# 32-step triangular inverses from two 16-step blocks in one lane, joined by small TensorE products

## The chip, the cores and the metric

The kernel runs on one core of a Trainium2 chip. The metric is the device time of one execution in microseconds (us), the median of several runs. Engines are named as in the profile: PE (TensorE matmul), PEld (its weight load), DVE (VectorE), ACT (ScalarE), POOL (GpSimd), SP (SyncE, which issues the DMAs).

## The reference, cut to what matters

```python
# 32 (batch, head) pairs, 768 steps, state 40 x 40, float32
for t in range(S):
    y[:, :, t] = einsum('bhd,bhde->bhe', r_t, state)
    Sa = einsum('bhde,bhe->bhd', state, a_t)
    state = state * w_t[:, :, None, :] - einsum('bhd,bhe->bhde', Sa, b_t) + einsum('bhd,bhe->bhde', v_t, k_t)
x = y as (3072 tokens, 320)
h = x @ w_in                                  # 320 -> 1024
solu = h * softmax(h)
x = layer_norm(solu) * g_ln @ w_out           # 1024 -> 320
h = x @ w2_in                                 # 320 -> 2048
out = (max(h, 0) + alpha * min(h, 0)) @ w2_out
```

The recurrence is computed in chunks of 32 steps. Within a chunk the update by `a` and `b` couples the steps, which makes a strictly lower triangular 32 x 32 matrix L for each chunk and head, and the kernel needs -(I + L)^-T of it. This inverse is what the change rewrites.

## The kernel before, in words

**Two phases.** `phase1` runs over 24 chunks of 32 steps (a slot each, `slot(g)`), two chunks to a window of 64 steps, and puts the first pair of products (the layers "h", "ptr", "po", "ptx") of earlier tokens between the chunks' own products. A second phase does the second pair of products (L1016 to L1039) and isn't touched.

**One slot.** In PE's order: `px` (L429), `pu` (L442, `stage_u`), `pf` (L465, `stage_uf`), `pst` (L477), `pg` (L520), `pss` (L497 or L500), `py` (L540), and between them the pieces of a queue of layer products: h (L575), ptr (L614), po (L628 to L630), ptx (L642). Each slot also prepares later windows: scans of the decays on DVE (L273 to L286, L277), scaled operands (L303 on DVE or POOL), XS (L312 on POOL), transposes pt (L401), and `gen1` (L326), which makes the matrices that become XS (L336) and L (L339, an ACT copy out of PSUM). For the first slots it decodes weight words: DVE L656 to L662, ACT L658 and L659, POOL L665, then an ACT cast L692.

**The inverse.** Four consecutive chunks (g//4 is the same) make 128 units of 32 x 32, (head, chunk) pairs, a unit to a lane. `inverse(W)` (L343 to L393) makes their inverses: a DVE transpose (L366) puts each unit into one partition, 31 rank-1 steps follow (L354 a multiplication into `tmp`, L358 an addition; L383 for the smallest ones), and a second transpose (L387) puts the result back into LMN, from where `pu` and `pf` read it as weights. W=0 is made ahead of slot 0, there with the rows from 10 on done by POOL (L354 and L358 on POOL). W+1 is made in the slots with g%4 = 2 and 3 (`inv_tasks`, first 18 pieces and the rest) and read from the next slot on. So there are six inverses: one ahead of slot 0, and one in each of the slot pairs 2/3, 6/7, 10/11, 14/15 and 18/19.

**What sets the order.** PE's order is that of the code. `pace` follows how many columns the array has lately worked on, by the code's own estimates, and where the count falls under a floor (`LEVELS`) takes a piece from the queue of layer products (`pop`); with an empty queue it takes a product of zeros: "busy" (L211, 128x512) in slots 0 to 3, "zero" (L182) later. `keep(24)` in slot 0 puts 24 "busy" products ahead of `pu`; the first waits for a memset of `busy` (L945), which is tied behind step KSTEP = 20 of the first inverse. The order of DVE, ACT, POOL and SP is set by the framework's scheduler, which weighs when operands are due; each engine then runs its list in order.

Of the kernel before, what the change touches and what calls it, by code (L numbers as in the profile page):

```python
# [21 lines left out]
KEEP0, KEEP1, KSTEP, KEND = 36, 24, 20, 4  # L22
# [10 lines left out]
PR, SM, TM = (10, 32), 2, 121  # L33
# [6 lines left out]
NI = 18  # L40
# [8 lines left out]
def tile_kernel(ctx: ExitStack, tc: tile.TileContext, w_fm, a0_fm, a_fm, kb_fm, r_fm, v_fm, v_tm,  # L49
                w1_in, w1_out, g_ln, w2_in, w2_out, alpha, ident_d, mask_d, r, k, v, w, a, b, w1_nat, out,  # L50
# [138 lines left out]
    def pace(dt, n):  # L189
        """follows dt us in which the array counts n columns: keeps those of the last SPAN us above the floor"""  # L190
        note(dt, n)
        floor, extra = LEVELS[min(st["slot"] // 4, 1) if st["slot"] != 4 else 2] if st["slot"] < NG - 4 else LEVELS[3]
# [4 lines left out]

    def idle(dt):
        """dt us in which the next products wait for other engines"""
        while dt > 0.1 and more():  # L200
            dt -= pop()
        note(max(dt, 0.0), 0)
# [39 lines left out]
    def check(w, pe):  # L242
        """counts what is out of range"""
# [70 lines left out]
    def gen1(g, half):  # L314
# [16 lines left out]
        c4, lraw = g % 4, st["lraw"]  # L331
# [11 lines left out]
    def inverse(W):  # L343
        M, NT = LMN[2 * W % 3], LMN[(2 * W + 1) % 3]

        P = PR[W > 0]

        def rank1(eng, tmp, s, rows):
            nt = 31 - s
            l = NT[:, s + 1:32, s]  # L350
            tv = tmp[:, 0:sum(b - a for a, b in rows) * nt].rearrange("p (i t) -> p i t", t=nt)
            for a, b in rows:
                sh = [128, b - a, nt]
                eng.tensor_tensor(out=tv[:, a - rows[0][0]:b - rows[0][0]], in0=M[:, a:b, s:s + 1].to_broadcast(sh),  # L354
                                  in1=l.unsqueeze(1).to_broadcast(sh), op=ALU.mult)
            for a, b in rows:
                o = M[:, a:b, s + 1:32]
                r = eng.tensor_tensor(out=o, in0=o, in1=tv[:, a - rows[0][0]:b - rows[0][0]], op=ALU.add)  # L358
            return r

        def pool_rows():
            for s in range(P, 31):
                rank1(nc.gpsimd, b1.tile([128, TM], F32, name="tmp2", tag="Yt"), s, [(P, s + 1)])

        def start():
            nc.vector.transpose(out=NT, in_=st["lraw", W].rearrange("p l t -> p t l"))  # L366
            if W:
                unit(M, nc.gpsimd)
            pool_rows()

        def step(s):
            n, nt = min(s + 1, P), 31 - s
            m = n // 2
            if n <= SM:
                ops = [(M[:, i, s + 1:32], NT[:, s + 1:32, s], M[:, i, s:s + 1]) for i in range(n)]
            elif nt <= SM:
                ops = [(M[:, 0:n, s + 1 + i], M[:, 0:n, s], NT[:, s + 1 + i, s:s + 1]) for i in range(nt)]
            else:
                st["step"] = rank1(nc.vector, b1.tile([128, 256], F32, name="tmp"), s,
                                   [(0, m), (m, n)] if W == 0 else [(0, n)])  # L380
                return
# [67 lines left out]
    def blank(p):  # L449
        """zeros in the rows between those of the two heads"""  # L450
# [201 lines left out]
    def decode(raw, e, m, o, scales=()):  # L652
        """scales: of column ranges, a factor for each row"""
# [14 lines left out]
    def words(src, scales=()):  # L668
        """words of 256 columns a row, or of 512 while the layers' tiles are free, decoded"""
# [126 lines left out]
    def inv_tasks(g):  # L796
# [26 lines left out]
    def tail_tasks(g):  # L823
        """of the tokens after the last chunk: transposes in, first products, second ones, transposes out"""
# [19 lines left out]
    def slot(g):  # L844
# [72 lines left out]
    def phase1():  # L917
# [8 lines left out]
        nc.sync.dma_start(out=mask, in_=mask_d)  # L926
        nc.sync.dma_start(out=ident, in_=ident_d)
# [13 lines left out]
        for i, (_, f) in enumerate(inverse(0)):  # L941
# [40 lines left out]
    def phase2(p2):  # L982
# [12 lines left out]
        def parts(f):  # L995
            """of the weights of 128 hidden units: the three row tiles in, and the rows out"""
# [52 lines left out]
        def limits():  # L1049
            """whether a decay is out of range"""  # L1050
# [202 lines left out]
    with ExitStack() as ms:  # L1253
# [99 lines left out]
```

## Time and profile before

| what | us |
|---|---|
| median of 3 runs (lowest to highest) | 1180.27 (1178.73 to 1182.65) |
| span of the profiled execution, first to last instruction | 1174.9 |
| PE busy in the span | 994.3 (85%) |
| DVE busy | 794.3 (68%) |
| ACT busy | 516.9 (44%) |
| POOL busy | 503.1 (43%) |
| mean granted TensorE clock | 0.896 |

The profile is of one execution, for which it gives the span from the first to the last instruction; the median of the runs is 5.4 us above it. In the rows, a timeline line is start, duration, engine, line, operation, what it writes and reads, count and, in brackets, how long the engine had been idle and which instruction ended that. A matmul of fp32 operands has two records, so 32 products of `pu` stand as x64. [...]

### The profile page before, as it was taken

How to read it: one execution, taken by the hardware profiler on the slowest of the kernel's cores; microseconds unless marked ns; L12 is line 12 of the kernel's file. 1: busy time of each engine (PE TensorE's matmuls, PEld its weight loads, DVE VectorE, ACT ScalarE, POOL GpSimd, SP SyncE). 2: the span in 40 equal slices, each digit the busy share in tenths (PEclk: the TensorE clock that was granted, in tenths of full speed). 3: DMA queues.
4: the chain of work that ended last, by engine and by line, in shares of the span. 5: the costliest groups of instructions: out<-in, count | busy, mean ns of one | idle time of the engine just before them, and what ended most of it. 6: DMA issues, size and time to landing. Idle time of an engine off the chain costs nothing.

```text
span 1174.9 us, 37092 instructions
## 1 busy us (share of the span) xinstructions
PE 994.3 (85%) x15913; PEld 802.3 (68%) x15934; DVE 794.3 (68%) x1610; ACT 516.9 (44%) x1198; POOL 503.1 (43%) x546
## 2 busy tenths in 40 slices
PE   6275686588878978797779878999999999999997
PEld 3233454467666767676667666788888888888886
DVE  8899689978988798879878966556333333333332
ACT  3324454476547663666465647655212121212121
POOL 6848565444434433443444326245233333333332
PEclk8676877789888987888889889999999999999999
DMA  5513344434333433343334333445202020201000
GB/s 167 140 43 94 82 145 123 105 108 126 86 93 107 125 78 93 107 125 78 96 89 119 106 90 94 119 144 169 55 1 73 1 73 1 72 1 48 1 23 15
DMA packets 105423, 100.24 MB, mean 85 GB/s; under 512 B 38244, under 2 KB 84644, under 8 KB 105252
## 3 DMA queue, kind: packets, MB, share of 16 engines
q1 hardware_dynamic: 105252, 97.80, 30.1%
q8 instruction: 127, 2.08, 0.8%
q14 instruction: 44, 0.36, 0.1%
HBM read 72.34 MB, written 25.43 MB: 83 GB/s over the span
## 4 chain that ended last, share of the span: by engine, by line
PE 44%; DVE 32%; ACT 6%; issue 6%; POOL 5%; DMA 5%; SPq 0%; POOLq 0%; DVEq 0%; ACTq 0%
PE ph L1016 13%; PE acc L1037 5%; DVE tmp L354 5%; PE acc L1039 5%; PE acc L1038 5%; DVE LMN L358 4%; PE h L575 4%; DMA kbf<-in_kb_fm_dram 3%; DVE VUS L482 2%; DVE KBS L508 2%; PE ph L1019 2%; DVE XS L336 2%; DVE H L277 2%; DVE P L582 1%; PE pf L465 1%
## 5 line engine op out<-in xcount | busy, mean ns | idle before, releaser
L1026 POOL TENSOR_TENSOR gll<-gt,gh 128x512 fp32r<-128x512 f32 (+1 forms) x112 | 127.1, 1153 | 239.0 <-ACT gh L1025 219.8
L595 DVE TENSOR_SCALAR gt<-ph,al 128x512 f32<-128x512 f32 (+1 forms) x112 | 71.1, 670 | 219.5 <-PE ph L1019 218.0
L1025 ACT CAST gh<-gt 128x512 fp32r<-128x512 f32 (+1 forms) x112 | 61.1, 560 | 268.9 <-DVE gt L596 268.6
L575 PE MATMUL h<-w1h,xt 128*128 128x512 f32 x240 | 104.4, 483 | 16.3 <-ACT h L584 16.3
L312 POOL TENSOR_TENSOR XS<-XS,H 40x512 f32<-40x512 f32 (+1 forms) x48 | 64.9, 1356 | 89.6 <-DVE H L277 53.7
L354 DVE TENSOR_TENSOR tmp<-LMN,LMN 128x87 f32<-128x87 f32 (+25 forms) x189 | 93.5, 506 | 3.4
L1037 PE MATMUL acc<-w2h,gh 128*128 128x320 f32 x288 | 94.0, 326 | 0.0
L1039 PE MATMUL acc<-w2h,gll 128*128 128x320 f32 x288 | 89.1, 309 | 0.3 <-POOL gll L1026 0.3
L1038 PE MATMUL acc<-w2l,gh 128*128 128x320 f32 x288 | 88.9, 309 | 0.0
L211 PE MATMUL busy<-busy 128*128 128x512 bf16 x200 | 61.8, 463 | 28.1 <-DVE tmp L354 22.9
L528 POOL TENSOR_TENSOR YS<-YS,mask 64x512 f32<-64x512 f32 x48 | 64.3, 1339 | 47.6 <-ACT YS L527 42.9
L358 DVE TENSOR_TENSOR LMN<-LMN,tmp 128x87 f32<-128x87 f32 (+25 forms) x189 | 77.1, 419 | 2.7
L575 PEld LDWEIGHTS h<-w1h,xt 128*128 128x128 f32 x240 | 50.0, 219 | 25.8 <-ACT h L584 18.5
L575 PE MATMUL h<-w1l,xt 128*128 128x512 f32 x144 | 67.5, 469 | 0.0
L628 PE MATMUL po<-wo1h,lnh 128*128 128x320 f32 x192 | 66.7, 348 | 0.5 <-DVE lnl L620 0.5
L596 DVE SCALAR_TENSOR_TENSOR gt<-ph,gt 128x512 f32<-128x512 f32 (+1 forms) x112 | 63.9, 606 | 0.5
L630 PE MATMUL po<-wo1h,lnl 128*128 128x320 f32 x192 | 61.5, 320 | 0.2 <-DVE lnl L620 0.2
L629 PE MATMUL po<-wo1l,lnh 128*128 128x320 f32 x192 | 61.5, 320 | 0.0
L211 PEld LDWEIGHTS <-busy 128*128 128x128 bf16 x221 | 23.2, 114 | 55.0 <-DVE busy L945 22.6
L1037 PEld LDWEIGHTS acc<-w2h,gh 128*128 128x128 f32 x288 | 54.1, 188 | 9.6 <-issue 7.4
L581 ACT ACTIVATE P<-h,sm 128x1024 f32<-128x1024 f32 x24 | 26.7, 1114 | 69.0 <-DVE sm L580 65.8
L1016 PE MATMUL ph<-w1h,w2h 128*128 128x512 f32 x180 | 56.6, 396 | 0.0
(214 smaller groups left out, 2718.9 us busy)
## 6 DMA issues: line engine op xcount, KB each, us to landing
kbf<-in_kb_fm_dram SPq DMA_DIRECT2D x24, 416.0 KB
x2d<-x SPq DMA_DIRECT2D x24, 320.0 KB
xd<-Y SPq DMA_DIRECT2D x24, 256.0 KB
xt<-xd SPq DMA_DIRECT2D x12, 512.0 KB
raw<-in_w_in_dram SPq DMA_DIRECT2D x20, 256.0 KB
wt<-in_w_fm_dram SPq DMA_DIRECT2D x24, 211.7 KB
raw<-in_w_in_dram SPq DMA_DIRECT2D x8, 512.0 KB
raw<-in_w_out_dram SPq DMA_DIRECT2D x16, 256.0 KB
```

What stands on the lines that cost most here:

```text
L211: nc.tensor.matmul(st["busy"], lhsT=busy[:, 0:128], rhs=busy, start=True, stop=True)
L312: (nc.vector if w < 2 and e in DA else nc.gpsimd).tensor_tensor(out=o, in0=o, in1=h, op=ALU.mult)
L354: eng.tensor_tensor(out=tv[:, a - rows[0][0]:b - rows[0][0]], in0=M[:, a:b, s:s + 1].to_broadcast(sh), in1=l.unsqueeze(1).to_broadcast(sh) ...
L358: r = eng.tensor_tensor(out=o, in0=o, in1=tv[:, a - rows[0][0]:b - rows[0][0]], op=ALU.add)
L575: nc.tensor.matmul(st["h"][:, ns], lhsT=l, rhs=r, start=j == 0, stop=j == len(ops) - 1)
L595: nc.vector.tensor_scalar(out=tmp, in0=h, scalar1=0.0, scalar2=al, op0=ALU.min, op1=ALU.mult)
L628: nc.tensor.matmul(po, lhsT=lh[:, k], rhs=wo1h[:, k], start=k == 0, stop=False)
L1016: nc.tensor.matmul(p, lhsT=l, rhs=r, start=j == 0, stop=False)
L1026: nc.gpsimd.tensor_tensor(out=gll, in0=t, in1=f32(gh), op=ALU.subtract)
L1037: nc.tensor.matmul(acc, lhsT=gh[:, cs], rhs=oh, start=f == 0, stop=False)
L1038: nc.tensor.matmul(acc, lhsT=gh[:, cs], rhs=ol, start=False, stop=False)
L1039: nc.tensor.matmul(acc, lhsT=gll[:, cs], rhs=oh, start=False, stop=f == K2 - 1)
```

## The change

The 32 x 32 triangle is cut into two diagonal blocks of 16 and the block between them. ACT writes L into a new tile GR (L339). Two half-size DVE transposes (L352, L353) bring both diagonal blocks of a unit into one lane of LMN. There, 14 steps work on both blocks at once, in place (L360 a multiplication, L363 an addition; 28 to 112 elements a lane). A masked copy (L368), a memset (L369) and a transpose (L370) make VT, and an ACT instruction (L371) VR from it. Then PE forms, per unit, `pv` (L376, 32x16 results, 128 of them), which ACT copies to A (LMN[2], L386), and `pn` (L376 too, 32x32 results, 128 of them), which ACT copies in two halves to LMN (L392), where `pu` reads the inverse. The first 16 pieces of `inverse` (all DVE work) go into the slot with g%4 = 2, the four PE pieces (left, left, join, join) into the slot with g%4 = 3; in slot 0 they stand between `keep(24)` and `stage_u`. POOL no longer takes rows of the first inverse. The memset that releases `keep(24)` is tied to step 2 instead of 20. A DMA of a constant `tri` (164 KB) and three POOL copies of it in `init` are new, and the memsets of LMN are gone.

```diff
-KEEP0, KEEP1, KSTEP, KEND = 36, 24, 20, 4
+KEEP0, KEEP1, KSTEP, KEND = 36, 24, 2, 4
...
     def init():
-        unit(LMN[0], nc.gpsimd)
+        for t, c, k in ((GR, 0, 0), (VR, 0, 1), (LMN[2], 16, 2)):
+            i = tri[:, 256 + 16 * k:272 + 16 * k].unsqueeze(1).to_broadcast([128, 32, 16])
+            nc.gpsimd.tensor_copy(out=t[:, :, c:c + 16], in_=i)
...
-                nc.scalar.activation(out=lraw[r:r + 32, c4 * 8:c4 * 8 + 8, :], in_=pg[o + 32:o + 64, :, e],
+                nc.scalar.activation(out=GR[r:r + 32, c4 * 8:c4 * 8 + 8, 47:15:-1], in_=pg[o + 32:o + 64, :, e],
                                      func=AF.Copy, scale=-1.0)
...
     def inverse(W):
+        X = LMN[W % 2]
+        L = X[:, 0:16, :].rearrange("p t (b a) -> p b t a", b=2)
+        A = LMN[2]
+        box = {}
 
         def start():
-            nc.vector.transpose(out=NT, in_=st["lraw", W].rearrange("p l t -> p t l"))
-            if W:
-                unit(M, nc.gpsimd)
-            pool_rows()
+            nc.vector.transpose(out=X[:, 15::-1, :], in_=GR[:, :, 32:48].rearrange("p l c -> p c l"))
+            nc.vector.transpose(out=X[:, ::-1, 16:32].rearrange("p s c -> p c s"),
+                                in_=GR[:, :, 16:32].rearrange("p l c -> p c l"))
 
         def step(s):
+            sh = [128, 2, 15 - s, s]
+            tmp = b1.tile([128, 128], F32, name="tmp")[:, 0:2 * s * (15 - s)]
+            tmp = tmp.rearrange("p (b t a) -> p b t a", b=2, a=s)
+            nc.vector.tensor_tensor(out=tmp, in0=L[:, :, s + 1:16, s:s + 1].to_broadcast(sh),
+                                    in1=L[:, :, s:s + 1, 0:s].to_broadcast(sh), op=ALU.mult)
+            o = L[:, :, s + 1:16, 0:s]
+            st["step"] = nc.vector.tensor_tensor(out=o, in0=o, in1=tmp, op=ALU.add)
 
         def fin():
-            st["fence"] = nc.vector.transpose(out=NT.rearrange("p l t -> p t l"), in_=M.rearrange("p i t -> p t i"))
-            st["NT", W] = NT
...
+            nc.vector.tensor_tensor(out=V.rearrange("p (b t) a -> p b t a", b=2), in0=L, in1=low, op=ALU.mult)
+            nc.vector.memset(V.rearrange("p (b t) a -> p b (t a)", b=2)[:, :, ::17], 1.0)
+            st["fence"] = nc.vector.transpose(out=VT.rearrange("p l a -> p a l"), in_=V.rearrange("p x a -> p a x"))
+            nc.scalar.activation(out=VR[:, :, 31:15:-1], in_=VT, func=AF.Identity, scale=tri[:, 320:321])
+
+        def units(p, lhsT, rhs, rows, ls):
+            for l in ls:
+                for q in range(0, 128, 32):
+                    nc.tensor.matmul(p[q:q + 32, l - ls[0], :], lhsT=lhsT[q:q + rows, l, 0:32], rhs=rhs[q:q + rows, l, :],
+                                     start=True, stop=True)
+                pace(0.11, 16)
+
+        def left(h):
...
+            units(p[:, 16 * h:16 * h + 16], GR, VT, 16, range(16 * h, 16 * h + 16))
+            if h:
+                nc.scalar.copy(out=A[:, :, 0:16], in_=p)
+
+        def join(h):
...
+            units(p, A, VR, 32, ls)
+            nc.scalar.copy(out=X[:, 16 * h:16 * h + 16, :], in_=p)
...
-        inv = [f for _, f in inverse(W + 1)]
-        return inv[:NI] if c4 == 2 else inv[NI:]
+        inv = list(inverse(W + 1))
+        return inv[:16] if c4 == 2 else inv[16:]
...
             keep(KEEP1)
+            for f in st["joins"]:
+                f()
         stage_u(g)
```

PE's program grows from 10256 to 12136 instructions: 768 `pv` and 768 `pn`, "zero" from 15 to 115 and "busy" from 221 to 293 (34 more in slot 0, 38 more in slot 3), their weight loads among them. Each of the slots 7, 11, 15 and 19 has 25 "zero" products where it had none.

**Place 1: PE in slot 0**, from `px` to `pf` (XP is the copy of `px`, LMN_161 and LMN_160 the tiles of the inverse). Before:

```order
L429 MATMUL px<-VUS_163,XS_150 32x40 x32
L211 MATMUL busy<-busy 128x512
...
L442 MATMUL pu<-XP,LMN_161 32x40 x4
...
L442 MATMUL pu<-XP,LMN_161 32x40 x28
L451 MATMUL pf<-D_148 32x256
```

Now:

```order
L376 MATMUL pv<-VT,GR 32x16 x4
...
L376 MATMUL pv<-VT,GR 32x16 x68
...
L376 MATMUL pv<-VT,GR 32x16 x56
L376 MATMUL pn<-VR,LMN_162 32x32 x12
...
L376 MATMUL pn<-VR,LMN_162 32x32 x68
...
L376 MATMUL pn<-VR,LMN_162 32x32 x48
L450 MATMUL pu<-XP,LMN_160 32x40 x16
```

Between the `keep(24)` and `pu` now stand the 128 `pv` and 128 `pn`, and where "..." stands among them 8 or 9 "busy" products of `pace`, 35 in all.

**Place 2: ACT in slot 0**, behind the copy of `px` (L666, L667 and L700 are the decode lines L658, L659 and L692 of before). Now:

```order
L440 COPY XP<-px 128x320
L371 ACTIVATE VR<-VT,tri 128x32x16
L251 ACTIVATE H,flags<-wt,lims 104x8x64 x2
L386 COPY LMN_162<-pv 128x32x16
L666 ACTIVATE wem<-wem,ebias 128x512
L667 ACTIVATE wem<-wem 128x512
L251 ACTIVATE H,flags<-wt,lims 104x8x64 x2
L700 CAST w1h<-wem 128x512
...
L392 COPY LMN_160<-pn 128x512
...
L392 COPY LMN_160<-pn 128x512
L454 COPY VUS_167<-pu 32x320
```

Before, the copy of `px` was followed by two decode instructions (L658, L659) and the copies of `pu`; now the three copies of the inverse stand among range checks (L251), decode instructions and casts.

**Place 3: DVE in slots 6 to 8**, the end of an inverse and the next window's scans (Yt is the result of a slot, XS the next operand). Before, ahead of slot 8's `pu`:

```order
L383 SCALAR_TENSOR_TENSOR LMN_161<-LMN_161,LMN_162 128x31
L387 STREAM_TRANSPOSE LMN_162<-LMN_161 128x32x32
L273 TENSOR_SCALAR wc<-wt 104x8x64
L274 MEMSET wc 104x9
L281 SCALAR_TENSOR_TENSOR F<-wc,D_148 104x520
```

Now, the end of the inverse is ahead of slot 6's Yt, and the scans ahead of slot 7's:

```order
L363 TENSOR_TENSOR LMN_160<-LMN_160,tmp 128x2x14
L368 TENSOR_TENSOR V<-LMN_160,tri 128x512
L369 MEMSET V 128x2x16
L370 STREAM_TRANSPOSE VT<-V 128x16x32
...
L552 TENSOR_TENSOR Yt<-py,H 104x512
...
L490 TENSOR_TENSOR VUS_167<-pst,VUS_168 40x320 x4
L273 TENSOR_SCALAR wc<-wt 104x8x64
...
L277 SCALAR_TENSOR_TENSOR H<-wc,Dx 104x520
...
L552 TENSOR_TENSOR Yt<-py,H 104x512
```

DVE's part of the inverse has moved from two slots into the first of them, and the scans from the beginning of slot 8 into slot 7.

## Rows read from the trace of the kernel before

**Rows 1.** The page: the chain that ended last, by engine and by line

```profile
PE 44%; DVE 32%; ACT 6%; issue 6%; POOL 5%; DMA 5%; SPq 0%; POOLq 0%; DVEq 0%; ACTq 0%
PE ph L1016 13%; PE acc L1037 5%; DVE tmp L354 5%; PE acc L1039 5%; PE acc L1038 5%; DVE LMN L358 4%; PE h L575 4%; DMA kbf<-in_kb_fm_dram 3%; DVE VUS L482 2%; DVE KBS L508 2%; PE ph L1019 2%; DVE XS L336 2%; DVE H L277 2%; DVE P L582 1%; PE pf L465 1%
```

**Rows 2.** Instructions by line, DVE: count, busy us, mean ns, idle before

```profile
L354 DVE TENSOR_TENSOR tmp<-LMN,LMN 128x87 f32<-128x87 f32 (+25 forms) x189 | 93.5, 506 | 3.4
L358 DVE TENSOR_TENSOR LMN<-LMN,tmp 128x87 f32<-128x87 f32 (+25 forms) x189 | 77.1, 419 | 2.7
...
L387 DVE STREAM_TRANSPOSE LMN<-LMN 128x1024 f32<-128x1024 f32 x6 | 12.0, 1999 | 0.3
```

**Rows 3.** Windows: length, busy (x) of PE, PEld, DVE, ACT, POOL, PEclk, DMA, GB/s

```profile
38.10:70.00 31.90, 8.79 (x87) 3.80 (x88) 30.72 (x118) 6.17 (x19) 20.56 (x50) 0.57 0.36 89
70.00:113.00 43.00, 25.81 (x557) 16.07 (x562) 42.33 (x63) 19.07 (x43) 30.00 (x19) 0.71 0.28 83
151.30:208.90 57.60, 44.57 (x990) 29.97 (x987) 52.87 (x99) 28.71 (x70) 31.40 (x30) 0.78 0.45 130
208.90:249.90 41.00, 25.75 (x649) 20.51 (x645) 35.59 (x76) 21.94 (x49) 18.44 (x20) 0.86 0.34 87
277.70:326.80 49.10, 42.99 (x1021) 34.44 (x1021) 45.65 (x95) 30.30 (x77) 19.94 (x26) 0.93 0.41 106
326.80:363.50 36.70, 27.01 (x645) 21.90 (x644) 33.17 (x73) 20.22 (x49) 15.14 (x18) 0.83 0.33 85
...
675.70:704.40 28.70, 22.79 (x516) 18.73 (x517) 18.02 (x42) 11.91 (x28) 6.69 (x9) 0.82 0.32 90
```

**Rows 4.** Timeline of PE in slot 0

```profile
62.10 7.73 PE L211 MATMUL busy<-busy 128*128 128x512 bf16 x23 [22.92 <-DVE tmp L354]
70.17 0.28 PE L442 MATMUL pu<-XP,LMN 32*32 32x40 f32 x8 [0.34 <-DVE LMN L387]
70.38 1.90 PE L211 MATMUL busy<-busy 128*128 128x512 bf16 x8
72.21 0.72 PE L442 MATMUL pu<-XP,LMN 32*32 32x40 f32 x56
...
73.07 0.80 PE L465 MATMUL pf<-LMN,XP 32*40 32x32 f32 x32
```

**Rows 5.** Timeline of DVE: the first inverse's ends, ahead of slot 0's pu

```profile
38.05 1.97 DVE L366 STREAM_TRANSPOSE LMN<-LMN 128x1024 f32<-128x1024 f32 x1 [1.20 <-ACT LMN L339]
...
67.94 2.08 DVE L387 STREAM_TRANSPOSE LMN<-LMN 128x1024 f32<-128x1024 f32 x1
```

**Rows 6.** Timeline of DVE in slots 7 and 8

```profile
301.27 0.68 DVE L544 TENSOR_TENSOR Yt<-py,H 104x512 f32<-104x512 f32 x1
...
331.11 0.36 DVE L354 TENSOR_TENSOR tmp<-LMN,LMN 128x112 f32<-128x112 f32 x1
331.50 0.27 DVE L358 TENSOR_TENSOR LMN<-LMN,tmp 128x112 f32<-128x112 f32 x1
...
333.70 1.98 DVE L387 STREAM_TRANSPOSE LMN<-LMN 128x1024 f32<-128x1024 f32 x1
```

**Rows 7.** Timeline of ACT in slot 0, around the decode

```profile
70.75 0.72 ACT L658 ACTIVATE wem<-wem,ebias 128x512 int32<-128x512 int32 x1 [26.32 <-DVE wem L656]
...
80.29 0.62 ACT L692 CAST w1h<-wem 128x512 fp32r<-128x512 f32 x1 [5.19 <-POOL wem L665]
```

**Rows 8.** Waits by pair: us in total, times, longest

```profile
PE pu L442 <- DVE LMN L387: 18.6, 5, 5.3
```

**Rows 9.** Timeline of PE: slot 4's longest wait, slot 8's pu, zeros

```profile
221.08 0.80 PE L575 MATMUL h<-w1h,xt 128*128 128x512 f32 x1 [11.39 <-ACT h L584]
...
246.77 1.24 PE L182 MATMUL zero<-D 104*128 104x512 bf16 x3 [1.43 <-ACT LMN L339]
...
335.82 1.29 PE L442 MATMUL pu<-XP,LMN 32*32 32x40 f32 x64 [4.53 <-DVE LMN L387]
```

**Rows 10.** Windows around slot 8's pu; columns as in rows 3

```profile
336.00:340.00 4.00, 4.00 (x104) 3.23 (x100) 3.96 (x7) 2.04 (x5) 0.00 (x0) 0.50 0.49 110
```

More of the change, by code (lines that the diff above doesn't have):

```diff
@@ L32 @@
 LAG, ND4 = 2, 4
-PR, SM, TM = (10, 32), 2, 121
 DA, KP = (1,), (1,)
@@ L39 @@
 DK = (1, 1)
-NI = 18
 ZF = (1, 1, 1, 1)
@@ L112, in tile_kernel @@
     LMN = [lm.tile([128, 32, 32], F32, name=f"LMN{i}") for i in range(3)]
+    GR = ca.tile([128, 32, 48], F32, name="GR")
+    VR = ca.tile([128, 32, 32], F32, name="VR")
+    VT = ca.tile([128, 32, 16], F32, name="VT")
+    tri = ca.tile([128, 321], F32, name="tri")
     VUS = [ca.tile([128, 2, 16, 40], F32, name=f"VUS{i}") for i in range(2)]
@@ L330, in gen1 @@
             return
-        c4, lraw = g % 4, st["lraw"]
+        c4 = g % 4
         for e in range(2):
@@ L338, in gen1 @@
                 r = q + 32 * pe
-                nc.scalar.activation(out=lraw[r:r + 32, c4 * 8:c4 * 8 + 8, :], in_=pg[o + 32:o + 64, :, e],
+                nc.scalar.activation(out=GR[r:r + 32, c4 * 8:c4 * 8 + 8, 47:15:-1], in_=pg[o + 32:o + 64, :, e],
                                      func=AF.Copy, scale=-1.0)
     def inverse(W):
[L344 to L359, printed above, removed]
@@ L371, in step @@
         def step(s):
[L372 to L381, printed above, removed]
@@ L382, in step @@
-            for o, x, f in ops:
-                st["step"] = nc.vector.scalar_tensor_tensor(out=o, in0=x, scalar=f, in1=o, op0=ALU.mult,
-                                                            op1=ALU.add)
-        def fin():
-            st["fence"] = nc.vector.transpose(out=NT.rearrange("p l t -> p t l"), in_=M.rearrange("p i t -> p t i"))
-            st["NT", W] = NT
-        yield 1.1, start
-        for s in range(31):
-            yield 0.15 + 2 * (s + 1) * (31 - s) / 960.0, (lambda s=s: step(s))
@@ new lines, in fin @@
+        def fin():
+            V = b1.tile([128, 32, 16], F32, name="V", tag="Yt")
+            low = tri[:, 0:256].rearrange("p (t a) -> p t a", a=16).unsqueeze(1).to_broadcast([128, 2, 16, 16])
+            nc.vector.tensor_tensor(out=V.rearrange("p (b t) a -> p b t a", b=2), in0=L, in1=low, op=ALU.mult)
+            nc.vector.memset(V.rearrange("p (b t) a -> p b (t a)", b=2)[:, :, ::17], 1.0)
+            st["fence"] = nc.vector.transpose(out=VT.rearrange("p l a -> p a l"), in_=V.rearrange("p x a -> p a x"))
+            nc.scalar.activation(out=VR[:, :, 31:15:-1], in_=VT, func=AF.Identity, scale=tri[:, 320:321])
@@ new lines, in units @@
+        def units(p, lhsT, rhs, rows, ls):
[5 more added lines that the diff above has]
+        def left(h):
+            if h == 0:
+                box["p"] = ps_at.tile([128, 32, 16], F32, name="pv", tag="at")
+            p = box["p"]
+            units(p[:, 16 * h:16 * h + 16], GR, VT, 16, range(16 * h, 16 * h + 16))
+            if h:
+                nc.scalar.copy(out=A[:, :, 0:16], in_=p)
@@ L395, in trans @@
+        def join(h):
+            ls = range(16 * h, 16 * h + 16)
+            p = ps_at.tile([128, 16, 32], F32, name="pn", tag="at")
+            units(p, A, VR, 32, ls)
+            nc.scalar.copy(out=X[:, 16 * h:16 * h + 16, :], in_=p)
+            st["NT", W] = X
+        yield start
+        for s in range(1, 15):
+            yield lambda s=s: step(s)
+        yield fin
+        for f in (left, join):
+            for h in range(2):
+                yield lambda f=f, h=h: f(h)
     def trans(w, q):
@@ L926, in phase1 @@
         nc.sync.dma_start(out=mask, in_=mask_d)
+        nc.sync.dma_start(out=tri, in_=tri_d)
         nc.sync.dma_start(out=ident, in_=ident_d)
@@ L940, in phase1 @@
             kb_load(2)
-        for i, (_, f) in enumerate(inverse(0)):
+        inv = list(inverse(0))
+        st["joins"] = inv[16:]
+        for i, f in enumerate(inv[:16]):
             f()
@@ L972, in early_w @@
         k = [b2.tile([128, KI + 2 * KO], F32R, name="kbf") for _ in range(2)]
-        m = [lm.tile([128, 1024], F32R, name=f"LMN{i}") for i in (NG // 2 % 3, (NG // 2 + 1) % 3)]
+        m = [lm.tile([128, 1024], F32R, name=f"LMN{i}") for i in (0, 2)]
         st["x20"] = lm.tile([128, 4, 256], F32R, name="XS0"), m[0][:, KI:]
@@ L1327, in _layout @@
     o['mask'] = (np.arange(32)[None, :] > (np.arange(128) % 32)[:, None]).astype(f32)
+    tri = np.zeros((128, 256 + 64 + 1), f32)
+    tri[:, :256] = np.tril(np.ones((16, 16), f32), -1).ravel()
+    i16, p = np.eye(16, dtype=f32), np.arange(128) % 32
+    tri[:, 256:272] = np.where(p[:, None] < 16, i16[p % 16], 0)
+    tri[:, 272:288] = -tri[:, 256:272]
+    tri[:, 288:304] = np.where(p[:, None] < 16, 0, i16[15 - p % 16])
+    tri[:, 320] = np.where(p < 16, 0, -1)
+    o['tri'] = tri
     for n in 'rkvwab':
@@ L1338 @@
     from concourse.bass_utils import run_bass_kernel_spmd as _run
-    nc = _bacc.Bacc("TRN2", target_bir_lowering=False, num_devices=1)
+    nc = _bacc.Bacc("TRN2", target_bir_lowering=False, num_devices=1, dynamic_dma_scratch_size=1024)
     lay = _layout(inputs)
```

16 lines of the change are left out of this document (2 added, 14 removed).

## Prediction

> **What bounds the kernel now.** I read the chain first, then the table by line, then windows by slot, then the timelines around the places where PE stood. In the chain [rows 1] the reader is to see that PE holds 44% and DVE 32%: the first phase isn't bound by one engine but by a chain that goes back and forth. The table by line shows the inverse [rows 2]: 189 multiplications and 189 additions, 93.5 + 77.1 = 170.6 us, and six closing transposes with 12.0 us; as many opening ones at 1.97 us [rows 5] make it 195 us, some 32 us per inverse. The windows [rows 3] then tell where that matters. From 38 to 70 us DVE is busy 30.72 of 31.90 us and PE only 8.79. From 70 to 113 us DVE is busy 42.33 of 43.00: still DVE. In slots 6 and 7 (277.7 to 326.8) both are nearly full: PE 42.99, DVE 45.65 of 49.10. In slot 8 (326.8 to 363.5) PE falls to 27.01 of 36.70. The timelines show why: pu of slot 8 waited 4.53 us for the closing transpose [rows 9], which ended at 335.7 [rows 6]; over the whole program pu waits 18.6 us in 5 such places [rows 8]. In the 4 us after that wait the granted clock is 0.50, the lower of its two levels [rows 10].
>
> **What the change takes from DVE.** An inverse now costs DVE two half transposes (half of 1.97 us each [rows 5], so 2.0), 28 small instructions, a masked copy of 512 elements (0.68, as Yt [rows 6]), a memset (0.1) and a 512-element transpose (1.0). The small ones have 28 to 112 elements. At 112 a multiplication takes 0.36 and starts 0.39 ahead of its addition, which takes 0.27 [rows 6]; all 28 at that would be 14 x (0.39 + 0.31) = 9.8 us. Ten of the fourteen pairs are smaller, so I take 0.3 each, 8.4 us. Sum 12.2 us against some 32, or 20 us less per inverse, 120 us in all. That isn't the gain: it counts only where DVE ends the wait.
>
> **What it adds to PE.** Per inverse 128 pv and 128 pn, and fillers that the pacing adds: 35 in slot 0, 38 in slot 3, 25 "zero" in each of slots 7, 11, 15 and 19. No row shows pv or pn. The nearest is pu, tiles of 32x32 too: 56 records, two per product, in 0.72 us [rows 4], 0.026 us per product. The far one is pf, 32x40: 32 records in 0.80 us, 0.05 per product [rows 4]. So 256 products take 6.6 to 12.8 us. I take 6.6, since pu has the same tile and the same four groups of lanes. A filler is 1.90 / 8 = 0.24 us [rows 4], or 1.24 / 3 = 0.41 for three zeros in a row [rows 9]; I take 0.24, since the many zeros here rotate through several buffers. 25 of them take 6.0 to 10.3 us. An inverse so adds 12.6 us to PE in the later slots, 23.1 at the worst.
>
> [...]
>
> **Slot by slot,** against the profiled span of 1174.9 us:
>
> *The start: +1.* A new DMA of 164 KB and three POOL copies of 512 elements stand ahead of the first inverse. POOL has no such row here; at up to 1 us each (half of the 1024-element transpose [rows 5]) they cost 0 to 3 us. They are covered as long as the matrices L come later than they do.
>
> *Slot 0: -17.* DVE's part begins at 38.05 and now ends at 50.3 instead of 70.0 [rows 5]. The 24 busy products, released at about 41 instead of 62.10 [rows 4], run at 7.73 / 23 = 0.34 us until 49. Then 128 pv and 17 fillers, 3.3 + 4.1 us, end at 57.7. The copy to A waits in ACT's list behind range checks of a window that has still to be loaded; I put it at 60.6. 128 pn with 18 fillers, 7.6 us, end at 68.2, the copy behind them lets pu begin at 68.6 against 70.17 [rows 4]. Pu itself gains 1.6 us. The gain lies elsewhere: from 50 to 70 DVE is free and does the scans and word decodes that fill 42.33 of the 43.00 us after 70 [rows 3]. ACT's first decode, which waited 26.32 us for DVE [rows 7], moves ahead too. DVE has 19.7 us less in the slot; I take 17 of it, since POOL's part of the decode stays (ACT's cast waited 5.19 us for it [rows 7]). The ends are -2 (only pu's own gain) and -20.
>
> *Slots 2 to 4: -9.* In slots 2 and 3 (57.60 us) PE gets 6.6 + 38 x 0.24 = 15.7 us on top of 44.57 [rows 3], which has 13.0 us of room; DVE's part of the inverse, now all in slot 2, puts the operands behind it off a little. I take +4. In slot 4, h waits 11.39 us for ACT [rows 9], behind DVE's part of the softmax, which stands in DVE's list behind the inverse; that goes with most of the inverse's tail: -13.
>
> *The steady slots: -3.* In each of the pairs 6/7, 10/11, 14/15 and 18/19 PE gets 12.6 us and has 49.10 - 42.99 = 6.1 us of room [rows 3], so +6.5; I take +7 for the wait of pv for VT. In slots 8, 12 and 16 I take -9 each: the 8.8 us from the slot's start at 326.8 to the end of the transpose at 335.7 [rows 3, 6] are DVE work that is gone; the wait of 4.53 [rows 9] goes with it, and with no such wait nothing lowers the clock to 0.50 behind it [rows 10]. The scans that followed the transpose are now ahead of slot 7's Yt. What is late next is the layer products' own operands and PE itself. Slot 20, 28.70 us with 22.79 of PE [rows 3], gives -4. Sum 28 - 27 - 4 = -3.
>
> The second phase: 0, none of its instructions changes.
>
> Sum +1 - 17 - 9 - 3 = -28: a span of 1147, and 5.4 us more for the median of runs, 1152 us.
>
> **The rivals.**
>
> *Nearly all that DVE loses is gained.* The two lines of the steps hold 5% and 4% of the chain [rows 1], about 106 us. For this: the low clock and the waits vanish together, so the pairs' 6 us overhang may be paid back. Then the pairs cost +2, slot 0 gives -20 and slots 2 to 4 give -14: 28 us less than the forecast, 1124 us. Against it: 42.99 of 49.10 us of PE in a pair leaves no room for 12.6 [rows 3].
>
> *The gain goes into ACT's list.* The copies of pn (slot 0) stand behind decode instructions that wait for POOL. If ACT stalls there as it does at 80.29 [rows 7], pu comes at 75 or later, the rest of slot 0 follows it, and the slot gives -2 instead of -17. With +10 instead of +7 in the pairs, the sum is -1: no change, 1179 us. For it: ACT works strictly in order, and pu, pf and the copies behind it are a chain. Against it: DVE, not pu, ends the waits after 70 [rows 3].
>
> *PE becomes the bound in the pairs, and it is slower.* The place is the end of slots 3, 7, 11, 15 and 19. Per inverse 12.6 us are in the sum; it turns at 28 / 5 = 5.6 us more, 18.2 per inverse. Products at pf's 0.05 with fillers at 0.24 make 18.8, 31 us more in five pairs, 1183; with zeros at 0.41 it is 23.1, 52 us more, 1204. In the middle, 1193 us. For it: pv and pn are more small products than any slot has now, and the fillers aren't needed by anybody. Against it: pu's row. What the pairs cost would then not be given back in slot 8, since there only the 4.53 us wait and the tail can go.
>
> **How the numbers follow.** A measurement of this kernel can tell 0.3%, 3.5 us. The forecast (1138 to 1166) has 0.52, the larger gain (1115 to 1138) 0.14, a smaller one between forecast and no change 0.10, no change 0.08, slower 0.16. So faster 0.76, same 0.08, slower 0.16. The range goes from 1122 to 1183: below it about 0.05 of the larger gain, above it most of the slower case. The unknown terms alone, products and fillers at their ends, and slot 0 from -2 to -20, lie within it except where they come together.
>
> **What would show each step.** In the profile after: DVE busy lower by some 120 us and the lines of the steps at 0.3 us or less apiece. pu of slot 0 at 67 to 70 us, slot 0's end at 94 to 98 instead of 113, with DVE busy from 50 on with scans. No wait of pu for DVE; none of 11 us for h in slot 4. Slots 6/7 at 55 to 57 us with PE over 53 busy, slot 8 at 27 to 28, its clock at 1.00 for most of it. pv and pn at 0.026 us apiece: at 0.05 or above the forecast falls. If slot 0 ends after 105, the second rival holds.

## The result and the profile after

The change is slower by a little: 1186.10 us (median of 20 runs, 1179.46 to 1196.46) against 1179.54 us for the kernel before in the same rounds (20 runs, 1174.96 to 1188.00). The ratio is 1.0059, 95% interval 1.0037 to 1.0082. I had forecast 1152 us, with a range up to 1183 and a chance of 0.16 for slower.

The profiled execution took 1194.91 us, 8.8 us above the median, and that of the kernel before had a span 5.4 us below its median, so a difference of the two profiles overstates the loss; what they show of where the time goes is read below together with other runs. The page of the change, busy time and chain (before: [rows 1]; "issue" is time in which an engine waited for nothing that the profile shows):

```profile
PE 1057.2 (89%) x19178; PEld 842.2 (71%) x19178; DVE 690.2 (58%) x1382; ACT 533.5 (45%) x1222; POOL 472.9 (40%) x495
...
PE 43%; DVE 7%; ACT 5%; issue 4%; POOL 2%; DMA 2%; SPq 0%; POOLq 0%; ACTq 0%; DVEq 0%
```

DVE lost 104 us of work, where 120 were forecast, and PE gained 63. (The shares of this chain add up to 63% only: it could be followed back to 440 us and no further, so they aren't to be set against the 98% of before.) The span grew by 18.2 us. Lengths of the stages in the two profiles, from windows that begin at the px of each slot:

| slots | before, us | after, us | difference |
|---|---|---|---|
| 0 and 1 | 113.2 | 98.0 | -15.2 |
| 2 to 5 | 126.4 | 131.3 | +4.9 |
| 6 to 9 | 113.1 | 117.5 | +4.4 |
| 10 to 13 | 118.1 | 125.1 | +7.0 |
| 14 to 17 | 117.2 | 125.2 | +8.0 |
| 18 to 21 | 104.9 | 111.1 | +6.2 |
| sum | 692.9 | 708.2 | +15.3 |

Over these windows PE's busy time went from 536.6 to 597.2 us and DVE's from 589.1 to 482.6. PE's idle time fell from 156.3 to 111.0. In these two executions 45 us of PE's waiting went and 61 us of PE's work came.

The windows of the change that answer to [rows 3] (length, busy time and count of PE, PEld, DVE, ACT, POOL, granted clock as a share of full speed, DMA share, GB/s): slot 0 to its pu, the rest of slot 0, slots 2 and 3, slot 4, slots 6 and 7, slot 8, slot 20:

```profile
38.50:70.80 32.30, 23.79 (x635) 12.39 (x635) 30.63 (x65) 13.53 (x35) 11.72 (x14) 0.84 0.45 120
70.80:99.40 28.60, 23.75 (x562) 15.10 (x563) 18.96 (x33) 13.83 (x29) 19.69 (x14) 0.88 0.31 86
136.50:202.40 65.90, 55.22 (x1550) 36.08 (x1539) 52.36 (x109) 33.21 (x78) 30.27 (x29) 0.91 0.41 117
202.40:241.30 38.90, 27.26 (x643) 22.71 (x643) 25.48 (x45) 19.70 (x45) 17.70 (x21) 0.78 0.37 105
267.80:330.20 62.40, 54.43 (x1573) 42.63 (x1563) 42.83 (x98) 35.54 (x84) 22.88 (x26) 0.94 0.36 95
330.20:361.40 31.20, 25.89 (x644) 21.53 (x643) 23.23 (x41) 18.80 (x46) 15.24 (x18) 0.86 0.34 86
...
701.90:722.20 20.30, 19.41 (x514) 16.32 (x511) 10.88 (x24) 10.05 (x26) 7.34 (x9) 1.00 0.44 120
```

Slots 6 and 7 took 62.4 us instead of 49.1, slot 8 31.2 instead of 36.7. The timeline of PE in slot 7 shows what stands there now:

```profile
298.28 0.65 PE L376 MATMUL pv<-VT,GR 16*32 16x16 f32 x56
...
309.47 0.49 PE L376 MATMUL pv<-VT,GR 16*32 16x16 f32 x36 [1.41 <-issue]
...
313.64 0.75 PE L376 MATMUL pn<-VR,LMN 32*32 32x32 f32 x64
...
314.87 1.90 PE L182 MATMUL zero<-D 104*128 104x512 bf16 x8
...
322.04 2.33 PE L182 MATMUL zero<-D 104*128 104x512 bf16 x10
```

A product is two records, so pv and pn take 0.65 / 28 = 0.023 us per product, and the zeros 0.24 each: close to the prices of the prediction, 0.026 and 0.24.

In slot 0 (against [rows 4]) pu starts at 70.81, no earlier than before, behind a wait of pn for the copy to A (3.19 us) and its own for the last copy to LMN (1.44 us):

```profile
41.58 7.04 PE L211 MATMUL busy<-busy 128*128 128x512 bf16 x24 [1.60 <-DVE busy L952]
50.47 0.25 PE L376 MATMUL pv<-VT,GR 16*32 16x16 f32 x8 [1.84 <-DVE VT L370]
...
52.48 1.33 PE L376 MATMUL pv<-VT,GR 16*32 16x16 f32 x136
...
60.23 0.54 PE L376 MATMUL pn<-VR,LMN 32*32 32x32 f32 x24 [3.19 <-ACT LMN L386]
...
70.81 0.49 PE L450 MATMUL pu<-XP,LMN 32*32 32x40 f32 x32 [1.44 <-ACT LMN L392]
```

But DVE began the scans at 50.2 instead of 69.9, and the slot ended at 99.4 instead of 113.0. In slot 4 the 11.39 us of [rows 9] are gone, and another wait stands there: the layer product po waits for lnl, one of its operands, as PE's timeline and then DVE's show:

```profile
221.62 0.61 PE L636 MATMUL po<-wo1h,lnh 128*128 128x320 f32 x1 [9.94 <-DVE lnl L628]
```

```profile
213.48 2.08 DVE L281 TENSOR_TENSOR_SCAN F<-wc,Dx 104x520 f32<-104x520 f32 x1
...
220.79 1.29 DVE L628 TENSOR_TENSOR lnl<-ptr,lnh 128x512 fp32r<-128x512 f32 x2 [1.53 <-POOL raw L673]
```

DVE's lnl, whose input ACT had ready at 212, now stands in DVE's list behind two windows' scans and a decode, and then waits 1.53 us for POOL.

pu's wait for DVE, 18.6 us in all before [rows 8], is gone as well, and here too another one came: pu now waits for XP, ACT's copy of px.

```profile
PE pu L450 <- ACT XP L440: 14.2, 8, 3.5
```

### The profile page after: what moved, and what is told of

It is laid out like the page before. It is cut to its first block, busy times and chain, and to the rows that moved or that the text cites. A ratio compares the mean times of both kernels' runs of the same rounds, so it can differ in the third digit from the quotient of the medians.

```text
span 1193.1 us, 43341 instructions
## 1 busy us (share of the span) xinstructions
PE 1057.2 (89%) x19178; PEld 842.2 (71%) x19178; DVE 690.2 (58%) x1382; ACT 533.5 (45%) x1222; POOL 472.9 (40%) x495
## 4 chain that ended last, share of the span: by engine, by line
PE 43%; DVE 7%; ACT 5%; issue 4%; POOL 2%; DMA 2%; SPq 0%; POOLq 0%; ACTq 0%; DVEq 0%
PE ph L1023 13%; PE acc L1044 5%; PE acc L1046 5%; PE acc L1045 4%; PE h L583 3%; PE ph L1026 2%; PE ptr L622 1%; PE po L636 1%; PE pf L473 1%; PE py L548 1%; PE pst L485 1%; PE po L638 1%; PE po L637 1%; DMA raw<-in_w_out_dram 1%; POOL YS L536 1%
## 5 line engine op out<-in xcount | busy, mean ns | idle before, releaser
L583 PE MATMUL h<-w1h,xt 128*128 128x512 f32 x240 | 100.6, 468 | 1.9 <-ACT h L592 1.9
L536 POOL TENSOR_TENSOR YS<-YS,mask 64x512 f32<-64x512 f32 x48 | 67.2, 1399 | 69.8 <-ACT YS L535 67.7
L211 PE MATMUL busy<-busy 128*128 128x512 bf16 x293 | 81.0, 427 | 2.9 <-DVE busy L952 1.6
L636 PE MATMUL po<-wo1h,lnh 128*128 128x320 f32 x192 | 69.4, 361 | 13.5 <-DVE lnl L628 13.5
L628 DVE TENSOR_TENSOR lnl<-ptr,lnh 128x512 fp32r<-128x512 f32 x48 | 32.6, 685 | 54.6 <-ACT lnh L627 52.9
L336 DVE TENSOR_TENSOR XS<-pg,mask 32x256 f32<-32x256 f32 x96 | 39.9, 416 | 38.6 <-ACT GR L339 33.6
L490 DVE TENSOR_TENSOR VUS<-pst,VUS 40x320 f32<-40x320 f32 x92 | 45.0, 489 | 29.6 <-PE pst L485 27.5
L673 POOL TENSOR_TENSOR dec<-em 128x256 f32<-128x256 f32 x36 | 28.8, 799 | 80.9 <-issue 21.1
L596 POOL TENSOR_TENSOR sm<-sm,half 128x1 f32<-128x1 f32 x24 | 13.7, 569 | 110.1 <-DVE sm L595 106.3
```

Source lines behind the costliest of these rows:

```text
L211: nc.tensor.matmul(st["busy"], lhsT=busy[:, 0:128], rhs=busy, start=True, stop=True)
L536: nc.gpsimd.tensor_tensor(out=y[q, e], in0=y[q, e], in1=mask[q].unsqueeze(1).to_broadcast([64, 16, 32]), op=ALU.mult)
L583: nc.tensor.matmul(st["h"][:, ns], lhsT=l, rhs=r, start=j == 0, stop=j == len(ops) - 1)
L636: nc.tensor.matmul(po, lhsT=lh[:, k], rhs=wo1h[:, k], start=k == 0, stop=False)
```

## The experiments

After the result I held theory A, which the expectations below work out for each run: the first inverse is worth what was forecast, the five later ones cost more on PE, in line, than DVE's relief gives back.

**The first inverse alone, and the later ones alone.** Two hybrids: the old and the new `inverse` in one program, each with its own tile for L.

```diff
-        inv = list(inverse(W + 1))
-        return inv[:16] if c4 == 2 else inv[16:]
+        inv = list(inverse_old(W + 1))
+        return inv[:NI] if c4 == 2 else inv[NI:]
```

Expected of this one:

> Only the first inverse (ahead of slot 0) in the new form, the five others in the old one on DVE alone. Theory A: slot 0 and 1 are 15 us shorter as in the profile of the change, and nothing else is lost: about 1165 us, faster than both kernels. Rival D (what slot 0 gains is lost again later, since DMAs or decoded weights are then late): 1177 us or more.

Measured: 1162.23 us, ratio 0.9865 (0.9817 to 0.9913). And the other way round (old first inverse with KSTEP 20, new later ones):

> Only the first inverse in the old form, the five others in the new one. Theory A: the steady pairs and their neighbours cost some 5 to 8 us net per window pair, and slot 0 gains nothing: about 1186 + 15 = 1200 us. Rival D: 1186 us, as the change itself.

Measured: 1203.49 us, ratio 1.0209 (1.0166 to 1.0252). So the first inverse gives 17 us and the later ones take 24; the two add up to the change's +7. Rival D falls: slot 0's gain isn't lost later.

**Without the fillers.** The call of `pace` in `units` is gone:

```diff
-                pace(0.11, 16)
```

> The change without the pacing between the pv and pn products: no filler there (15 zero and 221 busy products in all, as in the kernel before, where the change has 115 and 293), and the layer products are not drawn forward into the inverse's products. Theory A (the fillers are work that PE pays in line, nothing covers it): the four steady pairs lose 25 x 0.24 = 6 us each, slot 3 loses 38 x 0.24 = 9 us, slot 0 little; some 33 us less than the change, about 1153 us. Rival B (the fillers hold the clock up, and the time without them is lost to a clock of 0.50 in and behind the joins): the same as the change or slower, 1183 us or more. Rival C (the small products themselves and the waits around them are what costs): about 1175 us.

Measured: 1184.38 us, ratio 1.0045 (1.0017 to 1.0073): no different from the change, so theory A was wrong on the fillers. With 100 zeros and 72 busy products fewer, nothing is won. In slot 7, from pu to the end of pss, a stretch that holds all of pv and pn, this run without fillers has

```profile
291.20:319.50 28.30, 24.09 (x853) 20.17 (x852) 13.46 (x29) 12.25 (x28) 8.60 (x7) 0.62 0.36 93
300.00:316.00 16.00, 14.70 (x504) 12.25 (x506) 10.41 (x19) 3.60 (x8) 4.23 (x5) 0.50 0.15 41
```

and the change

```profile
297.60:325.70 28.10, 25.77 (x902) 19.41 (x901) 16.94 (x35) 15.24 (x32) 8.90 (x9) 1.00 0.31 80
```

The two stretches are about equally long. The granted clock in them is 0.62 against 1.00, with 0.50 over 16 us in the middle of the first. Slot 7 is the clearest case: over the whole of slots 7, 11, 15 and 19 the clock is 0.65, 0.68, 0.74 and 0.69 without fillers, and 0.94, 0.86, 0.77 and 0.85 in the change. And PE's waits in the run without fillers have a kind that the change hardly has:

```profile
PE pn L376 <- issue: 11.4, 8, 2.6
...
PE pv L376 <- issue: 9.5, 6, 2.2
```

The same two groups by line in the change, where "issue" stands at 1.4 and 2.3 us:

```profile
L376 PE MATMUL pv<-VT,GR 16*32 16x16 f32 x1536 | 19.2, 189 | 3.3 <-DVE VT L370 1.8 <-issue 1.4
L376 PE MATMUL pn<-VR,LMN 32*32 32x32 f32 x1536 | 18.8, 196 | 5.5 <-ACT LMN L386 3.2 <-issue 2.3
```

So rival B is right in its sum, and two things fit it: a lower clock and 17 us more of "issue" on pv and pn. How much each of them costs isn't shown. Taking away only some zeros told the same:

> The change with every other product in its place, but without the 15 zero products per pair that the pacing between pv and pn asks for (55 zero products instead of 115; the 10 per pair ahead of the last pss stay). Theory A: 60 x 0.24 = 14 us less than the change, about 1172 us. Rival B (they hold the clock): no less than the change, 1183 us or more.

Measured: 1185.06 us, ratio 1.0030 (1.0002 to 1.0059), as the change. The edit kept `pace` and dropped the product in `pop` where `units` had called it. Here the "issue" of pn came back, 12.4 us where the change has 2.3, though the mean granted clock of the profiled execution hardly moved (0.922, in the change 0.924; in slots 7, 11, 15 and 19 it was 0.81, 0.67, 0.95 and 0.80):

```profile
PE pn L377 <- issue: 12.4, 8, 2.2
```

**DVE's relief without PE's load.** The first inverse new; `left` and `join` return at once for the others (W is 0 for the first), so their products and copies are left out, and later chunks compute from meaningless values.

```diff
         def left(h):
+            if W:
+                return
...
         def join(h):
+            if W:
+                st["NT", W] = X
+                return
```

> The first inverse in the new form; of the five later ones only DVE's part (and ACT's VR). Their pv and pn products and the copies of these are left out, so what later chunks compute from them is meaningless. Against the run with the first inverse new and the others old (1162 us) this shows what the relief of DVE alone is worth. Theory A (the relief is worth what the prediction took for slot 4 and the slots 8, 12, 16 and 20, and PE's products in line are what eats it): 1162 - 44 = some 1118 us. Rival E (other waits take the place of pu's wait for DVE, as po's 9.9 us for DVE's lnl in slot 4 of the change): 1145 us or more.

Measured: 1138.47 us, ratio 0.9649 (0.9613 to 0.9684). DVE's relief is worth 1162.2 - 1138.5 = 24 us, not 44. (The profiled executions of these two runs are 2.3 and 6.8 us below their medians.) Slots 2 and 3, slot 4, slots 6 and 7, slot 8 and slot 20 with the old later inverses:

```profile
134.90:194.60 59.70, 46.09 (x997) 30.38 (x989) 53.96 (x98) 28.61 (x70) 26.92 (x27) 0.79 0.41 118
194.60:235.10 40.50, 27.02 (x644) 21.81 (x642) 34.70 (x75) 21.40 (x48) 17.75 (x20) 0.76 0.32 86
262.40:311.50 49.10, 43.65 (x1025) 35.37 (x1028) 45.66 (x96) 30.42 (x77) 19.91 (x26) 0.90 0.39 105
311.50:347.60 36.10, 25.88 (x648) 21.15 (x647) 32.59 (x72) 19.84 (x48) 14.79 (x18) 0.90 0.32 86
657.50:685.40 27.90, 21.97 (x515) 18.21 (x514) 18.05 (x42) 11.92 (x28) 6.58 (x9) 0.82 0.35 91
```

and with DVE's part of the new ones alone:

```profile
135.60:187.00 51.40, 40.57 (x986) 27.75 (x984) 44.10 (x88) 27.65 (x69) 26.89 (x25) 0.89 0.46 134
187.00:232.30 45.30, 26.14 (x651) 20.61 (x647) 29.82 (x56) 22.79 (x50) 18.05 (x20) 0.81 0.33 80
260.60:310.00 49.40, 42.81 (x1021) 35.31 (x1021) 40.40 (x93) 30.76 (x78) 19.05 (x24) 0.93 0.39 105
310.00:340.80 30.80, 24.23 (x648) 20.24 (x647) 20.82 (x46) 21.15 (x50) 15.96 (x18) 0.94 0.39 100
638.70:658.50 19.80, 19.41 (x512) 16.26 (x511) 10.18 (x23) 10.72 (x26) 6.44 (x9) 1.00 0.52 148
```

Slots 2 and 3 win 8 us, slot 8 5 and slot 20 8; slots 12 and 16, measured in the same way, win 3 and 1. The pair 6 and 7 wins nothing, and slot 4 loses 5: with the inverse off DVE's list, h there waits even longer for ACT, whose input P DVE now makes behind scans, a decode and four scaled operands. PE and DVE in slot 4 of this run:

```profile
202.85 0.79 PE L589 MATMUL h<-w1h,xt 128*128 128x512 f32 x1 [15.01 <-ACT h L598]
```

```profile
192.50 4.62 DVE L304 TENSOR_TENSOR kbf<-kbf,F 104x512 f32<-104x512 f32 x4
...
200.12 1.21 DVE L596 SCALAR_TENSOR_TENSOR P<-h,P 128x1024 f32<-128x1024 f32 x1
```

Rival E has the direction; the measured time (1138) lies between the two theories.

**PE's load without DVE's relief.** The same products and fillers at the same places of PE's order, read by nobody, beside the old inverses:

```diff
+        dum = list(inverse(g // 4 + 1)) if g % 4 == 3 and ni else []
...
+            while dum and 4 - len(dum) < 4 * x:
+                dum.pop(0)()
```

> The first inverse in the new form, the five later ones in the old form on DVE, and beside them the same pv and pn products with the same fillers as in the change, at the same places of PE's order; nobody reads them. Theory A (PE's part is paid in line): 12.2 us in each of four pairs and 15 in slots 2 and 3, 1162 + 64 = 1226 us less what falls into PE's waits for DVE there (some 5 us each): 1200 us. Rival E: PE's waits for the old inverse hide most of it, 1180 us or less.

Measured: 1219.06 us, ratio 1.0330 (1.0293 to 1.0366). The load costs 57 us beside the old inverses and 1186.1 - 1138.5 = 48 us beside the new. PE's busy time is 54 us longer here than with the old inverses alone, so PE's waits for DVE covered next to nothing of it. The two parts also act on each other: beside this load DVE's relief is worth 1219.1 - 1186.1 = 33 us, without it 24.

**Fillers without products.** The run with DVE's part alone, with the change's fillers put back:

```diff
-                for q in range(0, 128, 32):
+                for q in range(0, 128 if W == 0 else 0, 32):
```

> As the run with DVE's part of the later inverses alone (their pv and pn products and the copies of these left out), but with all the fillers of the change at their places in PE's order (115 zero, 293 busy products). Against that run (1138 us) it gives the fillers' own price where no small product stands between them. Theory A (the fillers' busy time is paid in line): 100 x 0.24 + 38 x 0.24 = 33 us, 1171 us; with the change at 1186 the products would then cost 15. Theory B (fillers raise the clock and so pay for themselves in any case): 1145 us or less, and the products cost the other 40.

Measured: 1172.25 us, ratio 0.9921 (0.9888 to 0.9954). The sum of theory A, but not by its mechanism alone. In this run zeros waited for ACT, whose copy of pg had to free their buffer, 19.6 us in 4 places, where all zeros of the change waited 2.7 us:

```profile
PE zero L183 <- ACT YS L543: 19.6, 4, 5.8
```

So the 34 us aren't a clean price of 138 fillers, and the split of the load into fillers and products stays open. What is shown: for the later inverses, no products and no fillers 1138, fillers alone 1172, products alone 1184 (the run without pacing, in which slot 0 has none either), both 1186. Either of the two costs most of what both cost.

**Spreading the products.** If 256 small products in one slot are the trouble, three slots should take them better. pv and pn of the units that slots 8 and 9 need stay in slot 7, the other half goes behind pu of slots 8 (pv) and 9 (pn):

```diff
+        if c4 < 2:
+            return [list(inverse(W))[17 + 2 * c4]] if W else []
...
-        return inv[:16] if c4 == 2 else inv[16:]
+        return inv[:16] if c4 == 2 else [inv[16], inv[18]]
```

> All six inverses in the new form, no fillers between the products, and the later ones' products spread: the units that the first two chunks of a window pair need in the slot with g%4 = 3, the other half of pv in the next slot and of pn in the one after it, each behind pu (64 to 128 products in a stretch, where the change has 256 in one slot). Theory F (what costs is that 256 small products stand in one slot: the clock falls to 0.50 among them and PE waits for its instructions, 21 us of such waits in the run without pacing): 1138 + 5 x 5 = about 1163 us. Theory A (each product is paid wherever it stands): 1138 + 48 = about 1185 us, as in the run without pacing.

Measured: 1195.54 us, ratio 1.0169 (1.0086 to 1.0253). And with the pacing:

> The same spread with the pacing of the change between the products (97 zero products instead of 115, but most of them now in other slots). Theory F: some 1138 + 5 x 9 = 1183 us, the fillers being paid. Theory A: 1185 us. If the fillers earn their time by the clock it comes out below the spread run without them.

Measured: 1209.89 us, ratio 1.0251 (1.0179 to 1.0323). Theory F falls: spread, they cost 11 us more than together, paced 24. In the first of these runs PE stood longer still on "issue":

```profile
PE pn L376 <- issue: 25.8, 12, 6.1
```

Why the shorter stretches waited longer here wasn't tried further.

**What slot 0 is bound by.** Without fillers between the first inverse's products (the others old):

> As the run with the first inverse new and the others old, without the fillers between the products of slot 0's inverse. In the run without pacing slots 0 and 1 took 88 us, with it 98 in the change. Theory A (the 35 fillers stand in front of pu, and slot 0's clock isn't worth them): 8 to 10 us less, 1153 us. Rival B (the clock): no change, 1160 us or more.

Measured: 1160.06 us, ratio 0.9826 (0.9792 to 0.9860); 2 us below the run with the fillers, which ran from 1159.97 to 1170.47, so no difference is shown. Its slots 0 and 1 took 88.5 us where the run with the fillers took 94.7, but slots 2 and 3 took 64.0 instead of 59.7: most of what was won there was lost behind it. This is the fastest version that computes everything, 19 us below the kernel before. Joining only half of the units ahead of pu:

> The first inverse new, the others old, no fillers between the products, and in slot 0 only the half of the units that slots 0 and 1 read is joined ahead of pu; the other half behind pf. Theory A (slot 0 is bound by DVE behind pu, as the prediction took it): no gain, 1158 to 1162 us. Rival G (pu's time sets slot 0's end): pu some 4 us earlier and the run at 1156 us or less.

Measured: 1167.50 us, ratio 0.9907 (0.9880 to 0.9935). pu came at 54 us instead of 63, and 7 us were lost. Slot 0 itself took 53.5 us instead of 57.6, but slot 1 took 36.6 instead of 30.9. So rival G falls in its sum, though an earlier pu did end slot 0 earlier; why slot 1 grew wasn't tried.

## Why the prediction was wrong

By its own steps, with the term and what the runs gave:

| step | predicted | measured | by |
|---|---|---|---|
| start and slot 0 | -16 | -17 | first inverse new alone |
| slot 4, slots 8, 12, 16, 20: DVE's relief | -13 - 27 - 4 = -44 | -24 | DVE's part alone |
| slots 2 and 3 and the four pairs: PE's load | +4 + 28 = +32 | +48 | the change against that run |
| sum | -28 | +7 | |

The two middle rows depend on the order in which the parts are taken. PE's load first, they are -33 for the relief and +57 for the load; either way the load outweighs the relief by 24 us.

*The start and slot 0* were right in size and in mechanism. pu gained nothing (70.81 against 70.17, where 68.6 was forecast, the wait of 3.19 us for A included), and yet the slot ended 13.6 us sooner: the gain came from DVE's scans and decode between 50 and 70 us, as DVE's busy time behind pu shows, 18.96 us where it was 42.33 [rows 3].

*"Has 6.1 us of room"* is the step that failed for the pairs. I took PE's idle time in slots 6 and 7 together as room for new work. The prices were about right (0.023 us per product, 0.24 per filler, 12.2 us per inverse). But pv and pn all stand in slot 7, and there only 24.80 - 22.62 = 2.2 us were idle; the other 3.9 lay in slot 6. Slots 6 and 7 before:

```profile
277.70:302.00 24.30, 20.37 (x511) 16.54 (x511) 21.51 (x43) 13.08 (x33) 8.76 (x12) 1.00 0.46 126
302.00:326.80 24.80, 22.62 (x510) 17.89 (x510) 24.14 (x53) 17.21 (x44) 11.18 (x14) 0.86 0.37 86
```

And even that wasn't used. Slot 7 with DVE's part alone:

```profile
281.70:310.00 28.30, 22.93 (x511) 18.87 (x510) 22.13 (x54) 19.08 (x48) 11.49 (x14) 0.88 0.31 78
```

and in the change:

```profile
288.60:330.20 41.60, 33.66 (x1052) 25.17 (x1052) 27.00 (x61) 23.86 (x54) 15.02 (x16) 0.94 0.31 77
```

PE's idle time didn't fall there, it rose from 5.4 us to 7.9. Slots 6 and 7 went from 49.4 us without the products to 62.4 with them, 13.0 us for 12.2 us of work, and the other three pairs grew by 15.5, 21.6 and 18.0. (The profiled execution of the change was long by 8.8 us over all its stages and the other one short by 6.8, so these four differences are somewhat too large; by the medians the load costs 48 us in all.) In the trace of the change PE's products of slot 7 come in the order of the code, and 5.6 of PE's 7.9 us of waiting there stand ahead of pu and at py, where it waits for ACT and POOL, and not among pv and pn. The longest of them:

```profile
291.60 0.58 PE L409 MATMUL pt<-ident,kbf 104*128 104x104 f32 x4 [2.18 <-ACT KBS L413]
293.86 0.55 PE L650 MATMUL ptx<-ident,xs 128*128 128x128 f32 x3 [1.69 <-ACT xs L641]
...
328.13 2.11 PE L548 MATMUL py<-YS,KBS 128*40 128x32 f32 x62 [1.41 <-POOL YS L536]
```

My reading is that pv and pn covered none of these waits because they don't stand at them, and put off the products behind them instead. That isn't shown: no run moved the products to the waits, and the one that spread them cost more (1195.5 us against 1184.4). The run with the old inverses fits: 57 us. In slots 2 and 3, where I had +4 (15.7 us of work for 13.0 of room), 59.7 us became 65.9: 8 us of relief, which I hadn't counted, and 14 of load.

*"Goes with most of the inverse's tail: -13"* is the step that failed in slot 4. The wait didn't go, it changed hands. What DVE did instead of the inverse was the scans and decodes that the scheduler had put later before (in the kernel before the first scan of that slot began at 220.46, behind DVE's P at 217.88), and they stand ahead of the layer's small instructions just as the inverse did: h waited 15.01 us in the run with DVE's part alone, po 9.94 us in the change. I named the place (what is late next) but not the instruction.

*Slots 8, 12 and 16* gave 5, 3 and 1 us where I had 9 each, slot 20 gave 8 where I had 4. pu's wait for DVE (4.53 us in slot 8) is gone there as forecast. The remainder of my 9 was DVE work that nothing waited for, as I read the waits; no run takes it alone. The clock, which was 0.50 in the 4 us after that wait [rows 10], is 1.00 from 336 to 352 us in slot 8 of the change and 0.50 from 354 to 358, so that over the slot it is 0.86, against 0.83 before [rows 3]. That the wait was what lowered it was my estimate; no run shows it.

The third rival was the right one in its outcome and its place, PE in the pairs. Its price was wrong: it wanted products at 0.05 us or zeros at 0.41 to turn the sum, and neither came, so that its 1193 us lie near the measured 1186 is luck. The sum turned with prices as forecast, because PE's idle time covered less of them than I had counted and DVE's relief was worth about half. The trace of the change gives 23 ns per product for pv and pn in slot 7 (56 records of pv, two per product, in 0.65 us, and 64 of pn in 0.75) and 20 ns for pv in slot 0 (136 records in 1.33 us). From these I estimate 5 to 6 us for 256 products, less than the 6.6 that I took and far from the 12.8 at pf's price.

## What to carry to other kernels

PE's idle time wasn't room for new work by itself here (13.0 us more for 12.2 us of work in slots 6 and 7): look where in the order such time lies, price moved work in full, and treat the idle time as a cover only where the order puts the work there. When an engine is relieved, look up what its list holds next at that place: here PE then waited behind that, 15.01 us at h in one run and 9.94 us at po in another. Where one program holds the same code in two situations, price them apart: here the rewrite gains 17 us where DVE is busy 30.72 of 31.90 us and PE 8.79 [rows 3], and loses 24 where PE is nearly full.

## What the runs showed of the hardware that I had not expected

In rows of very small products PE stood in waits that the profile doesn't explain. In the run without fillers pv and pn waited 20.9 us in 14 places for nothing that the profile shows ("issue"), 1.5 us apiece, and pss and pst behind them as well:

```profile
PE pss L504 <- issue: 6.6, 4, 1.9
PE pst L484 <- issue: 6.4, 6, 2.1
```

With fillers between them, which take 0.24 us for one product, pv and pn waited 3.7 us; with 60 of the zeros left out, pn alone waited 12.4. The DMA table, over the first 780 us, of the kernel before and of the change, has more packets of instructions for the longer program:

```profile
q8 instruction: 108, 1.77, 1.0%
```

```profile
q8 instruction: 132, 2.16, 1.2%
```

That PE waits for its own instructions would fit this (1.77 MB in 108 packets are 16 KB a packet, and a product of pv with its 16 rows has two records, as one of px with 104 rows has), but no run takes only that away, and it stays a guess. With the fillers both changed at once, the clock (1.00 against 0.62 from pu to pss in slot 7) and these waits, and the fillers cost about what they brought (1186.1 us with them, 1184.4 without).
